# Placing VectorE's single sums behind other products in the last three blocks of a sliding-window attention and gated feed-forward kernel

## The chip, the cores and the metric

The kernel runs on one core of a Trainium2 chip. The metric is device time in microseconds (us): the median of several executions. Of one further look, the profiled execution, there is a hardware trace.

## The reference

The reference is causal attention with a window of 128 positions and a linear distance bias, for 8 sequences of 576 positions with 8 heads of 64, and behind it a gated feed-forward block on the 4608 resulting rows of 512:

```python
scores = where((rel >= 0) & (rel < 128), q @ k.T / 8 - slope[h] * abs(rel), -1e9)
x = softmax(scores) @ v            # heads joined: 4608 x 512
g = x @ w_gate                     # w_gate, w_val: 512 x 1536
out = (g * sigmoid(g) * (x @ w_val)) @ w_out      # 4608 x 512, float32
```

## The kernel before

The 4608 rows are handled as nine blocks of 512 rows (0 to 8, `NBLK` is 9). Attention fills the first part of the time beside the feed-forward work; from about 247 us on only the feed-forward work of the last three blocks (6, 7, 8) is left, and the change lies there. Two things run interleaved in that stage, both written with Strassen's scheme of seven half-size products and sums in place of eight.

**The gate and value products of block n** (`gate_val_by_seven`, driven by `seven_steps`). The 1536 columns are taken in six units u = 0 to 5. Each unit consists of seven products named first to seventh (line 628, four matmuls of 128x256 each), accumulated into PSUM tiles gX, gY and gZ. What reads them: ScalarE copies behind first (L637), fifth (L643, into p5) and sixth (L657, into u2), and Silu behind second (L650) and fourth (L679). VectorE adds gY and u2 behind third (L664) and multiplies by the Silu to give the left half of hT (L665); it adds gX and p5 behind seventh (L671) and multiplies by the other Silu behind fourth (L680), which gives the right half of hT. Fourth accumulates into the same gX that L671 reads, so fourth can start only when L671 is done. The turn of products, with "before" meaning the unit before, is: first (now), seventh (before), fifth (now), sixth (now), fourth (before), second (now), third (now). The last unit of block 8 also does its own seventh and fourth.

**The output products of block n-1** (`strassen`, line 532, six matmuls of 128x256 a product, p or po), one product slipped in after every third step, in two passes t = 0 and 1 of seven products. They read hT and three sums S2, S3, S4 over six slices m of hT. VectorE's results from them are written at L536 and L547, ScalarE's at L541, L554, L560 and L575. A product into po waits, among others, for the VectorE read of the po before (L536).

**Single sums** are small VectorE operations of 128x512 in fp16 which are not done on the spot but put in a list `later` and taken out one by one: the sums of the gate and value weights (L597 to L600, for block 6's units, `gate_val_weight_sums`), the sums of the next block's x (`x_sums`) and the sums of hT (`sums(n, c)`), the last two both by `four_sums` in lines 485 to 488. The h sums come in three parts c = 0, 1, 2 for each block; part c needs units c and c + 3. In each part L485 gives S3 and needs only unit c; L486 adds in place the right half of unit c + 3 and therefore needs its L680; L487 gives S2, and L488 S4. The third product of the output pass (po from S2) needs, for its last two slices, L487 of part c = 2, the last one.

**The order** on TensorE is written out by hand in this stage (`manual_schedule(engines=ENGINES["pe"])`). On VectorE the recording layer orders the operations, but `one_later` says where a single sum stands:

```python
with tc.issue_after(anchor[0]):
    later.pop(0)()
```

so a sum comes no earlier than behind the VectorE operation that `anchor` holds. Before the change, that is the last product that made hT (L665 or L680; L427 in earlier blocks). In the last three blocks one sum is taken out at every step of a turn, two where the list is long or the step is early or late in its block (line 769).

Of the kernel before, what the change touches and what calls it, by code (L numbers as in the profile page):

```python
# [51 lines left out]
def kernel(  # L52
# [10 lines left out]
    nc = tc.nc  # L63
# [6 lines left out]
    NBLK = NTOK // 512  # L70
# [358 lines left out]
    def gate_val(n, m):  # L429
        c0 = 384 if (n, m) in acted else 0  # L430
        gate(n, m, wide(n, m, "g"), c0)
        yield
        val(n, m, wide(n, m, "v"), c0)
        yield
# [48 lines left out]
    def four_sums(a11, a12, a21, a22, s2, s3, s4):  # L483

        return [lambda: nc.vector.tensor_sub(s3, a11, a21),  # L485
                lambda: nc.vector.tensor_add(a21, a21, a22),  # L486
                lambda: nc.vector.tensor_sub(s2, a21, a11),  # L487
                lambda: nc.vector.tensor_sub(s4, a12, s2)]  # L488

    def at_once(fs):  # L490
        for f in fs:
            f()

    def sums(n, c):

        if n not in hsum:
            hsum[n] = [spool.tile([P, HM, 256], FP16, name=f"S{i}", tag=f"S{i}") for i in (2, 3, 4)]
        lo, hi = slice(2 * c, 2 * c + 2), slice(HM + 2 * c, HM + 2 * c + 2)
        a11, a12 = hT[n][:, lo, 0:256], hT[n][:, hi, 0:256]
        a21, a22 = hT[n][:, lo, 256:512], hT[n][:, hi, 256:512]  # L500
        s2, s3, s4 = (t_[:, lo, :] for t_ in hsum[n])
        return four_sums(a11, a12, a21, a22, s2, s3, s4)
# [106 lines left out]
    later, anchor = [], [None]  # L609

    def one_later():

        with tc.issue_after(anchor[0]):
            later.pop(0)()

    def gate_val_by_seven(n):

        x = xT[n]
        A11, A12 = x[:, 0:HK, 0:256], x[:, HK:NKB, 0:256]
        S1, A22 = x[:, 0:HK, 256:512], x[:, HK:NKB, 256:512]  # L620
        S2, S3, S4 = xsum.pop(n)
        hT[n] = hpool.tile([P, NMB, 512], FP16, name="hT", tag="hT")
        live = {}

        def product(dst, w, c0, a, start=False):
            for i in range(2):
                for kb in range(HK):
                    nc.tensor.matmul(dst[:, i, :], w[:, kb, c0 + i * P:c0 + (i + 1) * P], a[:, kb, :],  # L628
                                     start=(start and i == 0 and kb == 0),
                                     stop=(i == 1 and kb == HK - 1), skip_group_check=True)  # L630

        def first(u):
            X, Y = (ps_a.tile([P, 2, 256], FP32, name=i, tag="a", bufs=4) for i in ("gX", "gY"))
            Z = ps_f.tile([P, 2, 256], FP32, name="gZ", tag="gv")
            live[u] = X, Y, Z
            product(X, G1, 2 * u * P, A11, True)
            nc.scalar.copy(Z, X)  # L637

        def fifth(u):
            Y = live[u][1]  # L640
            product(Y, tsum[u][0], 0, S1, True)
            p5 = epool.tile([P, 2, 256], FP32, name="p5", tag="exc", bufs=5)
            nc.scalar.copy(p5, Y)  # L643
            live[u] += (p5,)

        def second(u):
            Z = live[u][2]
            product(Z, G2, 2 * u * P, A12)
            s = supool.tile([P, 2, 256], FP16, name="s1", tag="tt")
            nc.scalar.activation(s, Z, AF.Silu)  # L650
            live[u] += (s,)

        def sixth(u):
            X = live[u][0]
            product(X, tsum[u][1], 0, S2)
            u2 = epool.tile([P, 2, 256], FP32, name="u2", tag="exc", bufs=5)
            nc.scalar.copy(u2, X)  # L657
            live[u] += (u2,)

        def third(u):  # L660
            X, Y, Z, p5, u2, s = live[u][:6]
            product(Y, V2, 2 * u * P, S4)
            v_ = supool.tile([P, 2, 256], FP16, name="v1", tag="uu")
            nc.vector.tensor_add(v_, Y, u2)  # L664
            anchor[0] = nc.vector.tensor_mul(hT[n][:, 2 * u:2 * u + 2, 0:256], s, v_).ins  # L665

        def seventh(u):
            X, Y, Z, p5, u2, s = live[u]
            product(X, tsum[u][2], 0, S3)
            v_ = supool.tile([P, 2, 256], FP16, name="v2", tag="uu")  # L670
            nc.vector.tensor_add(v_, X, p5)  # L671
            live[u] += (v_,)

        def fourth(u):
            X, v_ = live[u][0], live[u][-1]
            del live[u]
            product(X, tsum[u][3], 0, A22)
            s = supool.tile([P, 2, 256], FP16, name="s2", tag="tt")
            nc.scalar.activation(s, X, AF.Silu)  # L679
            anchor[0] = nc.vector.tensor_mul(hT[n][:, 2 * u:2 * u + 2, 256:512], s, v_).ins  # L680

        return {f.__name__: f for f in (first, second, third, fourth, fifth, sixth, seventh)}

    def seven_steps():
# [21 lines left out]
    def ffn():  # L706

        for n in range(NBLK):
            if n > 1:
                parts = chain(strassen(n - 1, 0), strassen(n - 1, 1))  # L710
            if n == 1:
                for j in range(PRE):
                    for _ in project(0, j, ps_f, "po", 1):
                        yield 1.0
            if n == SEVEN_FROM:
                break
            for m in range(NMB):
                for half, _ in enumerate(gate_val(n, m)):
                    yield 1.0
                    if n > 1 and 2 * m + half in AT:  # L720
                        next(parts)
                        yield 0.75
                    if n > 1:
                        for _ in range(1 + (len(later) > 3)):
                            if later:
                                one_later()
                if n == 1:
                    if m in (4, 6, 8, 10):
                        for _ in project(0, m // 2 - 2, ps_f, "po", 1):
                            yield 1.0  # L730
                    if m in (4, 6, 8):
                        weight_sums(m // 2 - 2)
                if n > 0 and m >= 9:
                    (at_once if n == 1 and m < 11 else later.extend)(sums(n, m - 9))
                if n + 1 == SEVEN_FROM:
                    if m == SILU_AT:
                        attention_ends()
                        by_silu.update((n, i) for i in range(m + 1, NMB))
                    if m in (SILU_AT + 1, SILU_AT + 2):
                        later.extend(gate_val_weight_sums(m - SILU_AT - 1))  # L740
                    if m == SILU_AT:
                        later.extend(x_sums(n + 1))
            if n > 1:
                assert next(parts, 0) == 0
        ends = [strassen(NBLK - 1, t) for t in range(2)]
        final = ()
        for n, k, name, which in seven_steps():
            if k == 0 and n > SEVEN_FROM:
                assert next(parts, 0) == 0
                parts = chain(strassen(n - 1, 0), strassen(n - 1, 1))  # L750
            if n == SEVEN_FROM and k in (1, 3, 10, 17):
                later.extend(gate_val_weight_sums(2 + (k + 4) // 7))
            yield 0.5
            if k % 3 == 1 and k < 42:
                next(parts)
                yield 0.75
            if k == 20 and n + 1 < NBLK:
                later.extend(x_sums(n + 1))
            if k == 35:
                later.extend(sums(n, 0))  # L760
            if name == "fourth" and which is not None and which[1] > 3:
                if which == (NBLK - 1, 5):
                    at_once(final)
                else:
                    later.extend(sums(which[0], which[1] - 3))
            if n == NBLK - 1 and k == 40:
                final = sums(n, 2)
                later.append(final.pop(0))
            for _ in range(2 if len(later) > 4 or k >= 39 or k < 7 else 1):
                if later:  # L770
                    one_later()
            if n == NBLK - 1 and k == 41:
                next(ends[0])
                yield 0.75
        assert next(parts, 0) == 0 and not later

        for t in (1, 0, 1, 0, 0, 0, 1, 0, 0, 1, 1, 1, 1):
            next(ends[t])
            yield 0.75
# [230 lines left out]
```

## Time and profile before

| what | us |
|---|---|
| median of 4 runs | 348.25 |
| lowest and highest run | 347.92, 349.14 |
| the profiled execution's own time | 349.14 |
| its span in the trace | 347.40 |
| busy in the span: TensorE matmuls | 330.5 |
| busy in the span: VectorE | 277.8 |
| busy in the span: ScalarE | 207.9 |

The profiled execution is the slowest of the four: it lies 0.89 us above the median, and 1.74 us of its time lie outside the span. In the trace PE is TensorE's matmuls, PEld its weight loads, DVE VectorE, ACT ScalarE, POOL GpSimd, SP SyncE. The start of an instruction is when it runs, the second number is how long it takes until its result is complete; the next one on the same engine may start a little before that. The granted clock of TensorE is 0.999 of full speed over the whole span.

### The profile page before, as it was taken

To read this page: it belongs to the slowest core of one execution; us is meant where nothing else is said; L and a number is where in the kernel's file an instruction comes from. 1 tells how busy PE (TensorE), PEld (TensorE's weight loads), DVE (VectorE), ACT (ScalarE), POOL (GpSimd) and SP (SyncE) were. 2 spreads that over 40 slices of the span, in tenths; PEclk is the share of its full clock that TensorE was granted. 3 is DMA by queue.
4 is the path that set the end of the run, shared out by engine and by line. 5 is a ranking of instruction groups with operands and counts; after the bars stand their busy time and mean duration, and the time that the engine had idled before them with its cause. 6 is when DMAs were issued, how large, how long until landed. Compare 5 with 4: busy or idle time off the path is not lost.

```text
span 347.4 us, 7775 instructions
## 1 busy us (share of the span) xinstructions
PE 330.5 (95%) x2983; PEld 218.6 (63%) x2983; DVE 277.8 (80%) x652; ACT 207.9 (60%) x412; POOL 109.7 (32%) x136
## 2 busy tenths in 40 slices
PE   7999987999999999999999999899999989989995
PEld 4484444444456565666565665565788878878884
DVE  5578874999798669987899889989896867675583
ACT  3758674555766665756556465563567657656750
POOL 8967680738855176743016000000000000000000
PEclk9999999999999999999999999999999999999999
DMA  9999999999999999999949912030100101001014
GB/s 151 168 180 175 157 177 139 104 126 145 150 172 143 169 157 173 155 160 139 186 109 124 151 32 77 15 92 15 63 30 32 62 0 63 30 33 62 0 64 120
DMA packets 160037, 37.37 MB, mean 108 GB/s; under 512 B 147328, under 2 KB 155648, under 8 KB 160000
## 3 DMA queue, kind: packets, MB, share of 16 engines
q0 software_dynamic: 118336, 18.62, 86.0%
q1 hardware_dynamic: 40976, 17.64, 26.5%
q10 hardware_dynamic: 688, 0.62, 0.6%
q8 instruction: 23, 0.38, 0.5%
q14 instruction: 14, 0.11, 0.1%
HBM read 37.91 MB, written 9.44 MB: 136 GB/s over the span
## 4 chain that ended last, share of the span: by engine, by line
PE 67%; DVE 17%; DMA 8%; ACT 5%; issue 2%; POOL 1%; ACTq 0%; DVEq 0%
PE pv L397 14%; PE po L532 14%; PE pg L397 13%; PE gX L628 6%; PE av L345 4%; PE ps L278 3%; DMA wo_sb<-in_moe_w_out_dram 3%; DMA qn<-in_q_dram 3%; PE gY L628 3%; PE p L532 3%; PE po L451 2%; DVE hT L427 2%; ACT ex L284 2%; DVE v L671 1%; PE gZ L628 1%
## 5 line engine op out<-in xcount | busy, mean ns | idle before, releaser
L397 PE MATMUL pv<-xT,wv_sb 128*128 128x512 f16 (+2 forms) x320 | 76.5, 358 | 0.3 <-DVE hT L427 0.2
L397 PE MATMUL pg<-xT,wg_sb 128*128 128x512 f16 (+2 forms) x320 | 75.8, 358 | 0.3 <-DVE xT L373 0.2
L415 ACT ACTIVATE tt<-pg 128x512 f16<-128x512 f32 (+2 forms) x70 | 41.3, 590 | 50.1 <-PE pg L397 49.1
L284 ACT ACTIVATE ex<-ps 128x512 f16<-128x512 f32 x96 | 50.0, 604 | 11.3 <-PE ps L278 11.3
L416 DVE SCALAR_TENSOR_TENSOR uu<-tt,pg 128x512 f16<-128x512 f16 (+2 forms) x69 | 45.9, 666 | 12.5 <-ACT tt L415 12.2
L427 DVE TENSOR_TENSOR hT<-uu,pv 128x512 f16<-128x512 f16 (+2 forms) x70 | 46.6, 665 | 3.6 <-PE pv L397 1.6
L185 POOL DMA_DIRECT2D va<-in_v_dram x40 | 34.4, 863 | 37.5 <-PE av L345 30.5
L397 PEld LDWEIGHTS <-wg_sb 128*128 128x128 f16 x320 | 28.3, 98 | 24.1 <-issue 2.3
L397 PEld LDWEIGHTS <-wv_sb 128*128 128x128 f16 x320 | 28.3, 98 | 23.7 <-issue 2.6
L532 PEld LDWEIGHTS <-hT 128*128 128x128 f16 x384 | 36.8, 98 | 10.1 <-issue 1.1
L191 POOL DMA_DIRECT2D qn<-in_q_dram x39 | 33.5, 865 | 18.9 <-DMA va<-in_v_dram 13.9
L191 POOL DMA_DIRECT2D kn<-in_k_dram x39 | 33.4, 859 | 19.0 <-DMA kT<-kn 13.1
L532 PEld LDWEIGHTS <-S 128*128 128x128 f16 x288 | 27.5, 98 | 12.3 <-DVE S L487 3.5
L290 DVE TENSOR_TENSOR ex<-ex,m_reg 128x1024 f16<-128x1024 f16 x42 | 28.8, 687 | 4.6 <-ACT ex L284 4.4
L532 PE MATMUL po<-T,S 128*128 128x256 f16 x192 | 26.7, 273 | 2.4 <-DVE S L487 2.4
L348 DVE TENSOR_TENSOR x<-av,rec 128x256 f16<-128x256 f32 x72 | 28.4, 419 | 0.5
L532 PE MATMUL po<-T,hT 128*128 128x256 f16 x192 | 26.0, 273 | 0.0
L317 ACT ACTIVATE exc<-psc 128x512 f16<-128x512 f32 x40 | 21.4, 606 | 4.2 <-PE psc L313 4.1
L680 DVE TENSOR_TENSOR hT<-s,v 128x512 f16<-128x512 f16 x18 | 7.6, 425 | 18.0 <-ACT s L679 18.0
L345 PEld LDWEIGHTS <-ex 128*128 128x128 f16 x384 | 17.4, 97 | 4.7 <-issue 1.5
L345 PE MATMUL av<-va,ex 128*128 128x65 f16 x384 | 19.3, 193 | 0.7 <-ACT ex L284 0.7
L278 PE MATMUL ps<-qT,kT 64*128 64x256 f16 x192 | 16.5, 272 | 0.4 <-DVE qT L223 0.2
(134 smaller groups left out, 535.9 us busy)
## 6 DMA issues: line engine op xcount, KB each, us to landing
out_dram<-osb SPq DMA_DIRECT2D x32, 256.0 KB, 3.2
va<-in_v_dram POOLq DMA_DIRECT2D x32, 128.0 KB, 8.4
qn<-in_q_dram POOLq DMA_DIRECT2D x31, 128.0 KB, 8.2
kn<-in_k_dram POOLq DMA_DIRECT2D x31, 128.0 KB, 8.3
wg_sb<-in_moe_w_gate_dram POOLq DMA_DIRECT2D x6, 256.0 KB, 7.6
wv_sb<-in_moe_w_val_dram POOLq DMA_DIRECT2D x6, 256.0 KB, 7.9
wo_sb<-in_moe_w_out_dram POOLq DMA_DIRECT2D x2, 768.0 KB, 9.4
kn<-in_k_dram POOLq DMA_DIRECT2D x8, 64.0 KB, 7.3
```

Source lines behind the costliest of these rows:

```text
L185: nc.gpsimd.dma_start(va[rank][p0:p1, :, 0:D], src)
L191: nc.gpsimd.dma_start(t_[p0:p1], src)
L284: nc.scalar.activation(e[:, o:o + 2, :], banks[q4][par], AF.Exp, scale=scale)
L290: nc.vector.tensor_mul(e[:, o, :], e[:, o, :], reg[:, o, :])
L345: nc.tensor.matmul(av[:, j, :], w, val, start=(n == 0), stop=(n == len(todo) - 1))
L348: nc.vector.tensor_mul(x[:, 4 * half:4 * half + 4, :], av[:, :, 0:D], rec.broadcast_to([P, 4, D]))
L397: nc.tensor.matmul(ps[:, c0:c1], w[:, kb, ms], xT[n][:, kb, c0:c1], start=(kb == 0 and c0 == 0), stop=(kb == NKB - 1 and c1 == 512), skip_ ...
L415: nc.scalar.activation(tt, pg[:, c0:c1], AF.Tanh, scale=0.5)
L416: nc.vector.scalar_tensor_tensor(out=uu, in0=tt, scalar=one if (n, m) == PIN else 1.0, in1=pg[:, c0:c1], op0=ALU.add, op1=ALU.mult)
L427: anchor[0] = nc.vector.tensor_mul(hT[n][:, m, c0:c1], acted[(n, m)][1][:, c0:c1], pv[:, c0:c1]).ins
L532: nc.tensor.matmul(dst, a[:, m, cols], b[:, m, :], start=(start and m == 0), stop=(m == HM - 1), skip_group_check=True)
L628: nc.tensor.matmul(dst[:, i, :], w[:, kb, c0 + i * P:c0 + (i + 1) * P], a[:, kb, :], start=(start and i == 0 and kb == 0), stop=(i == 1 an ...
```

## The change

The number of operations is the same. Two more VectorE operations set `anchor`: the additions L664 and L671, so that a single sum may stand directly behind one of them. In the last three blocks a single sum is taken out only behind the fourth, fifth, sixth and second products (the steps first, third and seventh take one only late in a block or when the list is longer than six). Behind a product two are taken out when the list has more than three. The h sums of part c = 1 and the first of part c = 2 (L485) are put in the list at fourth of unit 4. The other three of part c = 2 (L486, L487, L488) are put ahead of all others at fourth of unit 5, and there two are taken out at once, in block 8 all three.

```diff
@@ third, seventh @@
-            nc.vector.tensor_add(v_, Y, u2)
+            anchor[0] = nc.vector.tensor_add(v_, Y, u2).ins
...
-            nc.vector.tensor_add(v_, X, p5)
+            anchor[0] = nc.vector.tensor_add(v_, X, p5).ins
@@ ffn, the loop over seven_steps() @@
             if k == 35:
                 later.extend(sums(n, 0))
-            if name == "fourth" and which is not None and which[1] > 3:
-                if which == (NBLK - 1, 5):
-                    at_once(final)
-                else:
-                    later.extend(sums(which[0], which[1] - 3))
-            if n == NBLK - 1 and k == 40:
+            if name == "fourth" and which is not None and which[1] == 4:
+                later.extend(sums(n, 1))
                 final = sums(n, 2)
                 later.append(final.pop(0))
-            for _ in range(2 if len(later) > 4 or k >= 39 or k < 7 else 1):
-                if later:
+            if name == "fourth" and which is not None and which[1] == 5:
+                later[:0] = final
+                for _ in range(2 + (which[0] == NBLK - 1)):
                     one_later()
+            elif name not in ("first", "third", "seventh") or k > 39 or len(later) > 6:
+                for _ in range(1 + (len(later) > 3)):
+                    if later:
+                        one_later()
             if n == NBLK - 1 and k == 41:
```

## The prediction

> **What bounds the kernel now.** I read the page's busy shares first (matmuls 95% of the span), then the stretches by stage from 247 us on, where the change lies, then the waits of PE, and last the timelines of PE and DVE side by side.
>
> ```profile
> 277.10:292.00 14.90, 13.85 (x126) 12.16 (x126) 9.06 (x21) 9.30 (x19) 0.00 (x0) 1.00 0.10 37
> ...
> 334.00:347.40 13.40, 9.37 (x82) 7.73 (x81) 6.61 (x17) 2.13 (x5) 0.00 (x0) 0.98 0.30 88
> ```
>
> Behind the stretch and its length stand busy PE, PEld, DVE, ACT and POOL, then the granted clock. PE is the bound; DVE has about a third of a stretch free, so single sums cost only where they stand in front of something PE needs. The waits of PE from 249 us on:
>
> ```profile
> PE po L532 <- DVE S L487: 2.0, 2, 1.0
> PE gX L628 <- DVE v L671: 1.0, 4, 0.3
> ```
>
> These understate the loss, as ends on PE are modelled. I measure a stall from start to start: a product of four matmuls takes 0.44 us (279.10 to 279.53), one of six 0.66 (277.57 to 278.22), and what is above that is lost. The PE timeline, at the places that matter:
>
> ```profile
> 256.37 0.60 PE L628 MATMUL gY<-xT,kT 128*128 128x256 f16 x4
> 256.87 0.82 PE L532 MATMUL po<-wo_sb,S 128*128 128x256 f16 x6
> 257.52 0.60 PE L628 MATMUL gX<-m_reg,kT 128*128 128x256 f16 x4
> 258.14 0.60 PE L628 MATMUL gX<-xT,kT 128*128 128x256 f16 x4
> ...
> 276.27 0.60 PE L628 MATMUL gX<-m_reg,kT 128*128 128x256 f16 x4
> 277.13 0.60 PE L628 MATMUL gX<-xT,m_c 128*128 128x256 f16 x4 [0.27 <-DVE v L671]
> ...
> 279.53 0.60 PE L532 MATMUL po<-T,S 128*128 128x256 f16 x4
> 281.15 0.39 PE L532 MATMUL po<-T,S 128*128 128x256 f16 x2 [1.02 <-DVE S L487]
> ...
> 333.22 0.60 PE L628 MATMUL gY<-m_reg,wv_sb 128*128 128x256 f16 x4
> 334.00 0.60 PE L628 MATMUL gX<-xT,m_c 128*128 128x256 f16 x4 [0.18 <-DVE v L671]
> ```
>
> Four places lose time. A (start of block 6): fourth at 253.53, 0.09 late; the S4 product at 256.87, 0.06 late, behind L536 (started 256.41, done 256.82); fourth at 258.14, 0.18, and at 262.95, 0.44 late (due 262.07 + 0.44): 0.77. B (end of block 6): fourth of unit 4 due 276.71, starts 277.13: 0.42; the S2 product's fifth matmul due 279.97, starts 281.15: 1.18; together 1.60. C, the same at 306 to 310: fourth 0.43, S2 1.17. D (end of block 8): fourth 0.34 (due 333.66), the two p products 0.09 (335.09 to 336.49 for 1.31), S2 0.14 (336.49 to 337.29 for 0.66): 0.57. In all 4.5 us. The DVE rows that explain B:
>
> ```profile
> 273.66 0.42 DVE L680 TENSOR_TENSOR hT<-s,v 128x512 f16<-128x512 f16 x1 [0.33 <-ACT s L679]
> 274.00 0.42 DVE L485 TENSOR_TENSOR S<-hT 128x512 f16<-128x512 f16 x1
> 274.45 0.42 DVE L486 TENSOR_TENSOR hT<-hT 128x512 f16<-128x512 f16 x1
> ...
> 276.39 0.69 DVE L671 TENSOR_TENSOR v<-gX,p 128x512 f16<-128x512 f32 x1
> 278.40 0.42 DVE L680 TENSOR_TENSOR hT<-s,v 128x512 f16<-128x512 f16 x1 [1.32 <-ACT s L679]
> 278.74 0.42 DVE L547 TENSOR_SCALAR osb<-p 128x256 f32<-128x256 f32 x1
> 279.07 0.42 DVE L485 TENSOR_TENSOR S<-hT 128x512 f16<-128x512 f16 x1
> 279.40 0.68 DVE L664 TENSOR_TENSOR v<-gY,u 128x512 f16<-128x512 f32 x1
> ...
> 280.67 0.42 DVE L487 TENSOR_TENSOR S<-hT 128x512 f16<-128x512 f16 x1
> ```
>
> They give all prices: a short operation delays the next by 0.335 (278.40 to 279.07 is two); an addition from PSUM by 0.605 (279.40 to L486 at 280.01); a sum that reads the result just before it starts 0.45 behind it (274.00 to 274.45), L665 straight behind its L664 0.80 (250.65 to 251.45); fourth starts 0.74 behind the start of L671 (276.39 to 277.13), the S2 product 0.48 behind that of L487 (280.67 to 281.15).
>
> **The change, part by part.** In the built program PE, ACT, POOL and SP issue the same instructions in the same order, so no DMA moves; VectorE has the same operations in another order, from block 6 on. So I walk that order with the prices above.
>
> *A.* VectorE's order becomes L671, four weight sums, L680, four weight sums, L664, L536, L665, L671. L671 starts once seventh is done (251.47 + 0.60, so 252.11) and no longer holds fourth: 0.09 gained. The four sums then end their turn at 254.04, and VectorE idles until ScalarE's Silu is done: L680 at 254.70. What is queued behind that wait pays: four sums (1.34) to 256.04 + 0.34, L664 at 256.38, L536 at 256.98, done 257.40. The S4 product, now due at 256.72, starts at about 257.45: 0.73 lost where 0.06 was. Fourth behind it is due 257.45 + 0.66 + 0.44 = 258.54, L671 is done by 258.33: the 0.18 goes. For the last one, ScalarE's Silu lets L680 go at 259.85; two weight sums, L664 at 260.86 and L665 at 261.66 follow, L671 starts at 261.99 and is done at 262.68, and fourth is due at 262.91 (258.54 and seven products of four and two of six): the 0.44 goes. Sum 0.73 for 0.77: 0.04 gained. The weight sums themselves are used late: the closest, L599 at 252.71, is read by the unit's sixth at about 258.1; the x sums over 10 us later. They are hidden by that work; should a weight sum be late, each costs its 0.335 once.
>
> *B and C.* Between L680 (bound to 273.66 by ScalarE, as before) and L671 there now stand L488 of part 0 as well, which stood in VectorE's idle 0.33 before: L671 is 0.335 later, fourth stalls 0.42 + 0.335 = 0.755. The next L680 moves along, to 278.735. Behind it the order is L547, L486, L664, L487: 0.335 for L680, 0.335, 0.335 and 0.605 put L487 at 280.345, and the S2 product at 280.82. Its fifth matmul, also pushed by 0.335, is due at 280.305: it stalls 0.515. L485, put ahead of L680, is covered by the 1.32 us wait for ScalarE; L665 comes behind L487, and what it writes is needed only when the next h sums begin (299.98). Sum 1.27 for 1.60: 0.33 gained, at C again: 0.66.
>
> *D.* Behind L680 (331.92) stood L485 twice, L486, L671: 1.34. Now L488, L485, L486, L671, with the tight pair: 0.335 + 0.335 + 0.45 + 0.335 = 1.46. Fourth is 0.12 later, stall 0.46, L671 at 333.38. Then L487, L664, L488, L665, L485, L680, L536, L486, L536, L487: 0.605 + 0.335 + 0.605 + seven times 0.335 puts the last L487 at 337.27 and the S2 product's fifth matmul at 337.75. PE wants it at 334.12 + 0.44 + 0.66 + 1.31 + the p products' 0.09 + 0.44 for four = 337.05: 0.70 lost where 0.14 was. So the second L536, put in front of L487, and the chain behind it are what PE waits for, not the sums moved forward. Sum 1.25 for 0.57: 0.68 lost. This second L536 must itself wait for its product (done 336.8, needed 336.94): a cover of 0.14, and every 0.1 us beyond it costs 0.1. Behind the S2 product VectorE idles before each result (0.2 to 1.2 us in the trace), so nothing else changes up to the last store.
>
> Sum: -0.04 - 0.66 + 0.68 = -0.02 us. On the profiled execution (349.14) that is 349.1; it was the slowest of the four, 0.89 above the median, and on the median 348.25 it is **348.2**. Less than 0.3% (1.04 us) of this kernel can hardly be told from no change.
>
> Two rules bear on this. The row above says that a sum waiting for the result just before it costs 0.45 in place of 0.335. The Trainium skill ("VectorE: DVE Perf Modes", The DRAIN you can't avoid) says that a semaphore between chained operations costs nothing extra; by it D's first stall would not grow and the sum would be -0.14. The granted clock stays at 1.00 in the stretch with a stall of 1.18 us. The Trainium skill ("TensorE: Matmul & The Clock Gate", A second HAM failure mode) warns that micro-idles between groups of matmuls make the clock fall; as an estimate from its 3.4 us window at half the clock, one such fall would cost 1.7 us, and the sum would be about +1.7. The changed kernel's longest stall is 0.76, so the row decides.
>
> **The rivals.** *Slower: the S2 product isn't released by L487.* If it waits for what stands behind it (L665, then L488, which is 0.67 later), the gains of 0.67 at S2 in B and C are gone while fourth's extra 0.335 stay: -0.02 + 1.34 = +1.32, 349.6. It decides from the point where L488's end (281.55 before) governs. Against it: the matmul started at 281.15. *Faster: the new waits of A and D don't arise*, because the S4 product isn't tied to L536 and L487 finds room before the second L536: -0.02 - 0.67 - 0.56 = -1.25, 347.0. For it: the waits of PE name only L487 and L671. Against it: 256.82 and 256.87 fit within 0.05. *Only D goes wrong further*: the second L536 waits up to one price of a product (0.66) longer: 348.9. *The places move but cancel elsewhere, or VectorE has more slack than I see*: the gains of B and C without D's loss, -0.70, 347.5.
>
> **How the numbers follow.** The forecast gets 0.70, the slower rival 0.09, the faster 0.08, the last two 0.07 and 0.06; these two stay within 0.3%, so same has 0.83. Nine stall terms, each read to 0.05 us, are worth up to 0.45; the runs spread 1.2 us around their median, half of it about 0.6. Together about 0.8 to either side, which also takes in the last two cases: 347.4 to 349.1. The first two rivals stay outside with 0.17.
>
> **What would show it.** In the changed trace: fourth of unit 4 about 0.75 late in blocks 6 and 7, S2 about 0.5 late, one new stall of 0.7 at the S4 product near 257.4 and one of 0.7 inside the last S2 product near 337; the last matmul within 0.2 us of before's. Wrong: S2 still 1.2 late (slower), or no stall near 257 and 337 (faster), or a granted clock below 1.00 between 247 and 334.

## The result and the profile after

The changed kernel takes 348.52 us (median of 43 runs), the kernel before 348.50 us (64 runs); the ratio is 1.0002 with a 95% interval of 0.9987 to 1.0017. No change can be told, and a change of more than 0.2% is excluded. Forecast were 348.2 and no change. Single runs of the kernel before lie between 347.53 and 351.46. The profiled execution took 348.80 us, its span 347.0.

Where so little moves, the whole time says nothing about the steps. A finer measure is the stage that the change touches: from the start of the first fifth product of block 6 (the first gY of that stage) to the start of the last output product, both from the PE timeline. It is 342.56 - 247.98 = 94.58 us before and 341.76 - 247.25 = 94.51 us after. Inside it the stalls have moved to other places. The waits of PE in the trace after, in the same stretch as before:

```profile
PE gX L628 <- DVE v L671: 1.5, 3, 0.6
PE po L532 <- DVE S L487: 1.2, 3, 0.5
PE po L532 <- DVE osb L536: 0.6, 1, 0.6
```

The waits for L671 have grown (1.0 before), those for L487 have shrunk (2.0) but are three now, and one for L536 is new. The PE timeline after, at the four places; a product's due time is the start of the one in front plus 0.44 (four matmuls) or 0.66 (six):

```profile
255.54 0.60 PE L628 MATMUL gY<-xT,kT 128*128 128x256 f16 x4
256.72 0.81 PE L532 MATMUL po<-wo_sb,S 128*128 128x256 f16 x6 [0.58 <-DVE osb L536]
...
275.49 0.60 PE L628 MATMUL gX<-m_reg,kT 128*128 128x256 f16 x4
276.69 0.60 PE L628 MATMUL gX<-xT,m_c 128*128 128x256 f16 x4 [0.60 <-DVE v L671]
...
279.09 0.60 PE L532 MATMUL po<-T,S 128*128 128x256 f16 x4
280.03 0.39 PE L532 MATMUL po<-T,S 128*128 128x256 f16 x2 [0.35 <-DVE S L487]
...
335.15 0.60 PE L532 MATMUL po<-T,S 128*128 128x256 f16 x4
336.27 0.39 PE L532 MATMUL po<-T,S 128*128 128x256 f16 x2 [0.52 <-DVE S L487]
```

The S4 product (the output product that reads the sum S4; S2 likewise) at 256.72 was due at 255.98: 0.74 late. Fourth, two products on, starts at 257.81 without a gap. Fourth at 276.69 is 0.76 late, the S2 product's fifth matmul at 280.03 is 0.50 late, and the last S2 product at 336.27 0.68.

| place | stalls before | predicted after | measured after |
|---|---|---|---|
| A, block 6 | 0.09 + 0.06 + 0.18 + 0.44 = 0.77 | 0.73 | 0.74 |
| B, block 6 to 7 | 0.42 + 1.18 = 1.60 | 0.755 + 0.515 | 0.76 + 0.50 |
| C, block 7 to 8 | 0.43 + 1.17 = 1.60 | the same | 0.76 + 0.50 |
| D, end of block 8 | 0.34 + 0.09 + 0.14 = 0.57 | 0.46 + 0.09 + 0.70 | 0.47 + 0.09 + 0.68 |
| all | 4.54 | 4.52 | 4.50 |

The gain at B and C (0.34 each) is spent at D (0.67).

The DVE timeline after shows the chains that the stalls come from, A first, then B, then the end of D:

```profile
253.97 0.43 DVE L680 TENSOR_TENSOR hT<-s,v 128x512 f16<-128x512 f16 x1 [0.56 <-ACT s L679]
...
255.65 0.68 DVE L664 TENSOR_TENSOR v<-gY,u 128x512 f16<-128x512 f32 x1
256.25 0.41 DVE L536 SCALAR_TENSOR_TENSOR osb<-po,p5s 128x256 f32<-128x256 f32 x1
...
272.88 0.42 DVE L680 TENSOR_TENSOR hT<-s,v 128x512 f16<-128x512 f16 x1 [0.50 <-ACT s L679]
273.22 0.42 DVE L488 TENSOR_TENSOR S<-hT,S 128x512 f16<-128x512 f16 x1
...
279.56 0.41 DVE L487 TENSOR_TENSOR S<-hT 128x512 f16<-128x512 f16 x1
...
335.13 0.41 DVE L486 TENSOR_TENSOR hT<-hT 128x512 f16<-128x512 f16 x1
335.46 0.41 DVE L536 SCALAR_TENSOR_TENSOR osb<-p,osb 128x256 f32<-128x256 f32 x1
335.80 0.41 DVE L487 TENSOR_TENSOR S<-hT 128x512 f16<-128x512 f16 x1
```

In A VectorE waits 0.56 for ScalarE in front of L680 and then does four weight sums (254.31 to 255.65) before L664 and L536; L536 is complete at 256.66 and the S4 product starts at 256.72. In B L488 of part 0 now stands behind L680, where before it stood ahead of it in VectorE's wait (272.91, L680 at 273.66), and L671 starts 3.08 behind L680 (275.96) in place of 2.73. At D the second L536 stands between L486 and L487; L487 is complete at 336.21 and the S2 product goes on at 336.27.

### The profile page after: what moved, and what is told of

Its sections match the earlier page's. It is cut to its first block, busy times and chain, and to the rows that moved or that the text cites. A ratio compares the mean times of both kernels' runs of the same rounds, so it can differ in the third digit from the quotient of the medians.

```text
span 347.0 us, 7775 instructions
## 1 busy us (share of the span) xinstructions
PE 329.6 (95%) x2983; PEld 218.2 (63%) x2983; DVE 278.1 (80%) x652; ACT 207.6 (60%) x412; POOL 109.7 (32%) x136
## 4 chain that ended last, share of the span: by engine, by line
PE 65%; DVE 15%; DMA 12%; ACT 3%; issue 3%; POOL 1%; ACTq 0%; DVEq 0%; POOLq 0%
PE po L532 15%; PE pv L397 12%; PE pg L397 12%; PE gX L628 7%; PE gY L628 3%; PE av L345 3%; PE ps L278 3%; DMA wo_sb<-in_moe_w_out_dram 3%; DMA qn<-in_q_dram 3%; PE p L532 2%; DMA wv_sb<-in_moe_w_val_dram 2%; DMA kn<-in_k_dram 2%; DVE hT L427 2%; PE gZ L628 2%; DVE ex L290 1%
## 5 line engine op out<-in xcount | busy, mean ns | idle before, releaser
L680 DVE TENSOR_TENSOR hT<-s,v 128x512 f16<-128x512 f16 x18 | 7.6, 425 | 18.6 <-ACT s L679 18.5
```

## The experiments

The theory: each stall of TensorE in this stage is the place of one VectorE operation in its queue, counted in the prices of the prediction, and nothing else. In all ten traces TensorE and ScalarE do the same work in the same order in this stage, and GpSimd does none. The rivals: the third output product (S2) is released by something behind its sum; a stall that is removed comes back elsewhere; or the stalls belong to ScalarE, PSUM tiles or stores. Every kernel below has the same operations as the two kernels, and is read by its stage (94.58 before, 94.51 after) and by its stalls.

**One part of the change alone, on the kernel before.** Only the part 2 sums are split (L485 early, the other three first at fourth of unit 5); rules and anchors are those of before.

```diff
-            if name == "fourth" and which is not None and which[1] > 3:
-                if which == (NBLK - 1, 5):
-                    at_once(final)
-                else:
-                    later.extend(sums(which[0], which[1] - 3))
-            if n == NBLK - 1 and k == 40:
+            if name == "fourth" and which is not None and which[1] == 4:
+                later.extend(sums(n, 1))
                 final = sums(n, 2)
                 later.append(final.pop(0))
+            if name == "fourth" and which is not None and which[1] == 5:
+                later[:0] = final
+                if n == NBLK - 1 and k > 7:
+                    at_once(later)
+                    later.clear()
```

> Before's rules for when a single sum is taken out, with one part of the change alone: the first h sum of part 2 (L485) comes ahead of the last unit's fourth and the other three directly behind it, ahead of all else; no new anchors. Theory (every stall of TensorE is set by where the released VectorE operation stands in its queue): in blocks 6 and 7 fourth of unit 5 stalls 0.75 (0.42 before) and the third output product 0.5 (1.18 before); places A and D stay as before; the stage from the first fifth product of block 6 to the last output product is 0.66 us shorter than before's 94.58, and the time -0.2%, 347.8. Rival (the third output product is released by what stands behind its last sum): it still stalls 1.2, fourth 0.75, the stage 0.67 longer. Rival (a stall that is removed comes back elsewhere in the stage): stage within 0.2 of before.

Measured: stage 343.79 - 249.89 = 93.90, 0.68 shorter. The PE timeline of this kernel at place B:

```profile
279.38 0.60 PE L628 MATMUL gX<-xT,m_c 128*128 128x256 f16 x4 [0.60 <-DVE v L671]
...
281.78 0.60 PE L532 MATMUL po<-T,S 128*128 128x256 f16 x4
282.72 0.39 PE L532 MATMUL po<-T,S 128*128 128x256 f16 x2 [0.34 <-DVE S L487]
```

S2 stalls 0.50 and fourth 0.76, A and D are as before. So this split alone is enough for the gain of B and C, and it also brings a later fourth with it; the rivals for S2 fall. The operation that makes fourth late is another one here, L485 of part 2 (278.31) straight ahead of L671 (278.64); in the changed kernel it is L488 of part 0, and L485 stands behind L671. The time, 348.2 us (ratio 0.9994, 0.9965 to 1.0023), is too coarse to show it.

**The two anchors alone, on the kernel before.**

```diff
-            nc.vector.tensor_add(v_, Y, u2)
+            anchor[0] = nc.vector.tensor_add(v_, Y, u2).ins
...
-            nc.vector.tensor_add(v_, X, p5)
+            anchor[0] = nc.vector.tensor_add(v_, X, p5).ins
```

> Before with the two new anchors alone (L664 and L671), lists and rules as before. Theory of the queue's order: VectorE's order changes only behind block 8's last L680; A, B and C stall as before (0.77, 1.60, 1.60); at the end fourth is about 0.1 late and the p products then wait 0.75 for L665; stage 94.9 us, 0.3 longer than before. Rival (the anchors are what moves the sums in all three blocks): A and B stall as in the changed kernel, stage 94.5.

Measured, a single execution: stage 94.91; A, B and C as before, then fourth 0.13 late and the p products 0.75, waiting for L665. That is 0.33 worse than before, all at D.

**The changed kernel without the two anchors** (the diff above in reverse).

> The changed kernel without the two new anchors. Theory of the queue's order: single sums change places with additions at some points, but at none that TensorE waits for; the eight stalls of the changed kernel stay as they are, 0.74, 0.76, 0.50, 0.76, 0.50, 0.47, 0.09, 0.68; stage 94.5. Rival (the anchors matter): a stall changes by 0.3 or more.

Measured, a single execution: stage 94.54 with the same eight stalls, each within 0.01. With the new lists the anchors bring nothing.

**The changed kernel without the early L485 in blocks 6 and 7.**

```diff
-                final = sums(n, 2)
-                later.append(final.pop(0))
+                if n == NBLK - 1:
+                    final = sums(n, 2)
+                    later.append(final.pop(0))
...
-                later[:0] = final
+                later[:0] = final if which[0] == NBLK - 1 else sums(which[0], 2)
```

> The changed kernel, but in blocks 6 and 7 all four part 2 sums go into the list only at fourth of unit 5, none ahead of it; block 8 as in the changed kernel. Theory of the queue's order: with L485 out of the list fewer sums are taken out behind fourth of unit 4, fourth of unit 5 isn't late at all in blocks 6 and 7, and the third output product, whose L487 has one more sum ahead of it, stalls 1.2; A and D as in the changed kernel; stage 94.6. Rival (the gain at the third output product comes from L680 being late, not from L485's place): the third output product stalls 0.5 as in the changed kernel.

Measured, a single execution: stage 94.57; fourth at B and C isn't late at all, S2 is 1.28 late. The two stalls together are 1.28 where the changed kernel has 0.76 + 0.50 = 1.26. The wait has only moved from one product to a later one: with fourth free, S2 has to wait for the whole queue. As the two were 1.60 before, the early L485 isn't needed for the gain at B and C: the new rules for taking sums out bring nearly the same gain without it.

**One more sum ahead of L680 of unit 4**, on the changed kernel: three taken out at fifth of the last unit (step 37).

```diff
-                for _ in range(1 + (len(later) > 3)):
+                for _ in range(3 if k == 37 else 1 + (len(later) > 3)):
```

> The changed kernel, but at fifth of the last unit of each block three sums are taken out in place of two, so that L488 of part 0 comes ahead of L680 of unit 4 again, in VectorE's wait for ScalarE. Theory of the queue's order, price 0.335 for one short operation: fourth of unit 5 stalls 0.42 in place of 0.76 in blocks 6 and 7, the third output product 0.5 as in the changed kernel; at the end fourth 0.1, but then the p products wait 0.4 for L665 and the third product 0.7 still; stage 0.7 us shorter than 94.51; the time -0.2%, 347.8. Rival (these stalls are bound by ScalarE or by PSUM tiles, not by the one short operation): fourth still 0.7 late in blocks 6 and 7.

Measured: stage 93.84, 0.67 shorter than the changed kernel; fourth at B and C 0.42 and 0.43 late, S2 0.51 and 0.50, at the end 0.13, 0.39 and 0.67. The one short operation is worth 0.335 at each of B and C, as priced. The time, 348.6 us where 347.8 was expected, is again too coarse: the ratio to before is 0.9984 (0.9953 to 1.0016).

**The weight sums of place A moved**, on the changed kernel.

```diff
-                for _ in range(1 + (len(later) > 3)):
+                for _ in range(0 if n == SEVEN_FROM and k in (11, 12) else 1 + (len(later) > 3)):
```

> The changed kernel, but at fourth of unit 0 in block 6's second turn and the step behind it no weight sum is taken out; they follow at the next steps. Theory of the queue's order: the four weight sums that stood between L680 and L664 are what held L536 and through it the S4 product; its 0.74 goes, no new stall comes, B, C and D stay; stage 93.8. Rival (the S4 product is held by its PSUM tile's other reader or by ScalarE, not by L536): it stays 0.7 late, stage 94.5.

Measured, a single execution: stage 93.80, 0.71 shorter; the 0.74 is gone, B, C and D are the same within 0.01. The DVE timeline of this kernel at A, with nothing between L680 and L664:

```profile
253.83 0.42 DVE L680 TENSOR_TENSOR hT<-s,v 128x512 f16<-128x512 f16 x1 [0.56 <-ACT s L679]
254.18 0.68 DVE L664 TENSOR_TENSOR v<-gY,u 128x512 f16<-128x512 f32 x1
254.78 0.41 DVE L536 SCALAR_TENSOR_TENSOR osb<-po,p5s 128x256 f32<-128x256 f32 x1
```

L536 starts 0.95 behind L680 in place of 2.28 (253.97 to 256.25 in the changed kernel), and the S4 product no longer waits for it.

**Place D alone**, on the changed kernel: at the end of block 8 L486 and L487 of part 2 stand directly behind the last L680.

```diff
-            if name == "fourth" and which is not None and which[1] == 4:
+            if n == NBLK - 1 and k >= 39:
+                if k == 39:
+                    c1, c2 = sums(n, 1), sums(n, 2)
+                    later.extend((c1[0], c2[0], c1[1], c1[2], *c2[1:], c1[3]))
+                for _ in range({39: 2, 41: 1, 43: 9}.get(k, 0)):
+                    if later:
+                        one_later()
+            elif name == "fourth" and which is not None and which[1] == 4:
...
-            if name == "fourth" and which is not None and which[1] == 5:
+            if n == NBLK - 1 and k >= 39:
+                pass
+            elif name == "fourth" and which is not None and which[1] == 5:
```

> The changed kernel with another order of the last block's end only: behind the last unit's fourth the part 2 sums L486 and L487 come directly behind L680 and ahead of both L536. Theory of the queue's order: the 0.47 stall at block 8's last fourth and the 0.09 in the p products go, the third output product keeps 0.25 to 0.3 in place of 0.68; stage 0.9 us shorter than the changed kernel's 94.51; A, B and C as in the changed kernel; the time -0.27%, 347.6. Rival (the end is set by the output stores or by the second L536's own product, not by the sums): stage less than 0.3 us shorter.

Measured: stage 93.59, 0.92 shorter; one stall of 0.31 is left at D. The time is 347.4 us; the ratio to before is 0.9973 (0.9939 to 1.0008). Its DVE timeline at D, where L486 and L487 stand in pairs (parts 1 and 2):

```profile
333.11 0.42 DVE L680 TENSOR_TENSOR hT<-s,v 128x512 f16<-128x512 f16 x1
333.44 0.75 DVE L486 TENSOR_TENSOR hT<-hT 128x512 f16<-128x512 f16 x2
334.11 0.75 DVE L487 TENSOR_TENSOR S<-hT 128x512 f16<-128x512 f16 x2
...
335.45 0.41 DVE L536 SCALAR_TENSOR_TENSOR osb<-p,p1s 128x256 f32<-128x256 f32 x1
```

Both L536 now stand behind the sums, and no stall of TensorE comes from that.

**All four places.** Sums go into the time in which VectorE waits for the Silu behind fourth, that is behind seventh, four at a time; and L664 of the next unit is held behind the last L487.

```diff
...
+            if name == "third":
+                hold[0] = None
+            if name == "fourth" and which is not None:
+                if which[1] == 3:
+                    later.extend(sums(which[0], 0))
+                if which[1] == 4:
+                    c1, c2 = sums(which[0], 1), sums(which[0], 2)
+                    later.extend((c1[0], c2[0], c1[1], c1[2]))
+                    later.extend(c2[1:] + c1[3:] if n == NBLK - 1 else c1[3:] + c2[1:])
+                if which[1] == 5:
+                    while later:
+                        with tc.issue_after(anchor[0]):
+                            ins = later.pop(0)().ins
+                        if len(later) == (2 if n == NBLK - 1 and k > 7 else 1):
+                            hold[0] = ins
+            if n == SEVEN_FROM and k < 7:
                 for _ in range(1 + (len(later) > 3)):
                     if later:
                         one_later()
+            if name == "seventh" and which is not None:
+                for _ in range(1 if which == (NBLK - 1, 5) else 4):
+                    if later:
+                        one_later()
+            elif name == "fourth" and len(later) > 6:
+                one_later()
...
-            anchor[0] = nc.vector.tensor_add(v_, Y, u2).ins
+            with (tc.issue_after(hold[0]) if hold[0] else ExitStack()): anchor[0] = nc.vector.tensor_add(v_, Y, u2).ins
```

> All four places at once, on the changed kernel: sums are taken out mainly behind seventh (four at a time, while VectorE waits for the Silu behind fourth), part 0 of the h sums a unit earlier, part 1 and the first of part 2 behind the last unit's seventh, L486 and L487 of part 2 directly behind its L680 and ahead of L664. Theory of the queue's order: of 4.5 us of stalls 0.5 are left; stage 90.5 us; the time -1.15%, 344.5. Rival (the sums only fill time that TensorE loses anyway, to weight loads, PSUM tiles or ScalarE): stage within 1 us of 94.5, the time within 0.3% of before.

Measured: 344.59 us (median of 6 runs), ratio to before 0.9871 (0.9833 to 0.9909): 1.3% faster than before, and each of its runs is faster than every run of either kernel. Stage 338.66 - 248.06 = 90.60; stalls of 0.14, 0.14 and 0.32 are left, and the waits of PE in that stretch name none. The PE and then the DVE timeline of this kernel at B:

```profile
275.57 0.60 PE L628 MATMUL gX<-m_reg,kT 128*128 128x256 f16 x4
276.00 0.60 PE L628 MATMUL gX<-xT,m_c 128*128 128x256 f16 x4
...
278.41 0.97 PE L532 MATMUL po<-T,S 128*128 128x256 f16 x6
279.21 0.60 PE L628 MATMUL gX<-m_c,kT 128*128 128x256 f16 x4
```

```profile
277.38 0.42 DVE L680 TENSOR_TENSOR hT<-s,v 128x512 f16<-128x512 f16 x1 [0.16 <-ACT s L679]
...
278.05 0.41 DVE L486 TENSOR_TENSOR hT<-hT 128x512 f16<-128x512 f16 x1
278.50 0.43 DVE L487 TENSOR_TENSOR S<-hT 128x512 f16<-128x512 f16 x1
```

The rival falls. Fourth is on time (276.00 is 275.57 + 0.44) and the S2 product is one piece of six that takes 0.80 in place of 0.66. The wait for ScalarE in front of L680 has shrunk from 1.32 us before to 0.16, because the sums now stand in it. The 0.14 that is left fits L487 too: it is complete at 278.93 (278.50 + 0.43), and the S2 product's last two matmuls, which take 0.22 ahead of the next product at 279.21, go at about 278.99.

## Why the prediction was right

*The bound.* That the stalls of this stage are places in VectorE's queue is shown for 3.9 of the 4.5 us: with the same operations, and TensorE and ScalarE in the same order, the stage took from 90.60 to 94.91 us. The 0.6 that no order removed fit the end of L487, but were not tested.

*A, B, C, D.* Each new stall came within 0.02 us of its working: 0.74 for 0.73, 0.76 and 0.50 for 0.755 and 0.515, 0.47 and 0.68 for 0.46 and 0.70. The predicted -0.02 us for the whole stands against -0.07 by the stage and -0.04 by the table's stalls. The number alone would show little: the gains at B and C, 0.68 together, and the loss at D, 0.67, cancel, and the forecast of 348.2 rests on a median of four runs that lay 0.25 below that of 64. In A the walk also said that the stalls of 0.18 and 0.44 go; they went. One sign, the last matmul within 0.2 us of before's, holds only when counted from the start of the stage (94.51 for 94.58): in the times of the two traces it starts at 341.76 and 342.56, as the stage begins 0.73 earlier in the one after.

*The label.* The prediction speaks of "fourth of unit 4" at B and C. It is the fourth of unit 5, taken in the next block's first turn: behind the output product of 275.18 stand fifth and sixth of the next block's unit 0 and then this fourth, whose weights (m_c) are the last unit's. The L680 at 273.66 is that of unit 4, the one at 278.40 that of unit 5. The times, and so the sum, belong to the right instructions.

*The covers.* The weight sums and x sums were never waited for. The cover of 0.14 for the second L536 at D held: its product's wait doesn't show in the DVE row at 335.46.

*The two rules.* The price of 0.45 for a sum behind its own input was seen again (278.05 to 278.50 in the last kernel, 0.335 between sums that don't depend on each other), so D's first stall grew by 0.13, as the rows said, and not by nothing, as the other rule had it. The granted clock stayed at 1.00 in every stretch from 247 to 334 us, with gaps of up to 0.76 us here and 1.28 in the kernel without the early L485, and in the changed kernel also from 334 to 342, where the stall of 0.68 lies; the fall of the clock that the prediction priced at 1.7 us did not come.

*The rivals.* The slower one falls: S2 goes on 0.06 behind the end of L487 (280.03 for 279.56 + 0.41). The faster one falls in both halves: the S4 product is tied to L536 (its 0.74 goes when L536 comes earlier), and L487 found no room before the second L536. The two others fall too: the second L536 at D starts 0.33 behind L486, one price, so it didn't wait for its product, and D's loss came in full, 0.67 for 0.68. The spread of 1.2 us, taken from four runs, was too small (3.9 us over the 64 runs).

What the prediction did not look for is how much was still to be had: all of the 4.5 us but 0.6 could be removed by order alone.

## What to carry to other kernels

When small operations fill the gaps of a side engine, ask for each one which operation stands behind it in the queue and who waits for that one; a sum is free in front of an operation that waits for another engine anyway, and costs its full price (0.335 us here) in front of one that the bounding engine waits for. A gain at one product can be cancelled at a later one, as the queue in front of the last needed sum has to be worked off in any case, so walk the queue up to the end of the stage before adding up. When the expected change is smaller than the spread of the runs, measure the stage in the trace from start to start.

## What was not expected of the hardware

The stage repeats far better than the program. Its length came out at 94.51 and 94.54 in two programs with the same stalls, while the time at which it begins ran from 246.82 to 249.89 us over the ten traces, with the same instructions in front of it. In eight of the ten traces the granted clock between 40 and 60 us is 1.00; there the busy time of PE in that stretch and the start of the stage add up to 265.0 to 265.1 us in six (17.04 + 247.98 before, 17.80 + 247.25 after, 18.20 + 246.82 with place D alone) and to 265.4 in two. That fits a loss of TensorE there which moves everything behind it, but no run tests it. In the other two, the split alone and the changed kernel without the anchors, the clock in that stretch is 0.91, and the sum is 266.5; why it was lower was not tried.

The idle time that the profile prints for PE understates a stall by nearly the same amount each time: 1.02 is printed where the start-to-start loss is 1.18, 0.58 for 0.74, and 0.52 for 0.68.
